# A convolution with batch norm and SiLU: the first weight chunk's three taps loaded in quarters, one behind each of twelve x loads

## The chip, the cores and the metric

The kernel runs on one NeuronCore of a Trainium2 chip. The metric is the device time of one execution in microseconds (us). Beside the timed runs there is one profiled execution, whose trace gives the instructions of each engine, the waits between them and the DMA packets.

## The reference

```python
def reference(x, w, mean, var, g, b):      # x: 2 x 2048 x 1024, w: 3 x 1024 x 1024, bf16
    K = 3
    P = K // 2
    S = x.shape[1]
    xp = jnp.pad(x, ((0, 0), (P, P), (0, 0)))
    y = sum(jnp.einsum('bsc,cd->bsd', xp[:, k:k + S, :], w[k]) for k in range(K))
    inv_std = 1.0 / jnp.sqrt(var + 1e-5)
    y = (y - mean) * (g * inv_std) + b
    return _silu(y)
```

It is a convolution of width 3 along the sequence, over 1024 input and 1024 output channels, for two batches of 2048 positions; then a per-channel scale and shift, and SiLU.

## The kernel before

The convolution is computed in a transformed domain: six outputs of a channel come from eight inputs, with eight products where the direct form has eighteen. A tile is six output positions; a batch has 342 tiles. Each of the eight transformed inputs (j = 0 to 7) is multiplied by its own transformed weights.

**Input side.** A batch is cut into 17 windows of up to 21 tiles: windows of 128 rows of x (256 KB) and a last one of 33 rows. `load_window` (L205) loads one on SP's DMA queue; window 0 of each batch comes in two loads (L211, L212), the others in one (L215). `transform` (L218) turns a window into the transformed domain with TensorE (PE) matmuls against a small constant matrix `Rm` (L225), eight a window for batch 0, and casts the result from PSUM to `T_sb` on ScalarE (ACT, L239) or VectorE (DVE, L241). The pool `xwin` has ten buffers, so a load waits, late in a batch, until PE has read the window ten before it.

**Weight side.** Output channels come in eight chunks of 128. A chunk needs the three raw taps (tap 0, 1, 2: each 128 partitions x 8 channel blocks x 128 columns, 256 KB) and six sums of them, `wts` (the tiles `uch`). j = 0 and j = 7 use raw taps 0 and 2; j = 1 to 6 use the sums. For chunk 0, GpSimd (POOL) makes them: `pair_sum` (L163) adds taps 0 and 2, plain or scaled, `scale_weights` (L149) scales a tap, and `pair_tap` (L173) adds or subtracts tap 1. POOL's order is that of the code: sum, scale tap 2, sum, scale tap 0, sum, then the six products, with tap 1 first read by the first of these. `load_chunk` (L90) loads one tap of one chunk, and its rows in memory are 256 bytes long.

**Order.** Batch 0's loop over 17 windows does nothing on PE but the transforms. Then comes batch 1's loop: between its transforms the matmuls (L250) of the first unit (chunk 0, batch 0) are woven in, about one for every group of two or three transforms, 52 of 64 in all, in the order j = 7, 1, 3, 2, 4, 5, 0, 6. The other fifteen units (a chunk and a batch each) follow, and an output is transposed by DMA and stored on SP's queue behind them. The order on each engine is that of the code; the tile framework adds the waits. All these loads go through SP's one queue. The framework has eight semaphores for DMAs, used in turn, so a load also waits until the one eight places before it has landed.

In batch 0's loop the three taps of chunk 0 are loaded behind windows 3 (tap 0), 5 (tap 2) and 13 (tap 1), each by one load:

```python
            if wi in (3, 5, 13):
                load_chunk(0, {3: 0, 5: 2, 13: 1}[wi])
```

POOL's sums of taps 0 and 2 are written behind window 7, the six products behind window 13.

Of the kernel before, what the change touches and what calls it, by code (L numbers as in the profile page):

```python
# [37 lines left out]
def kernel(  # L38
# [10 lines left out]
    nc = tc.nc  # L49
    B, S, C = x.shape  # L50
    D = w.shape[2]
    P = 128
    CT = C // P
# [19 lines left out]
    w_all = w.rearrange("k (ct p) d -> p k ct d", p=P)  # L73
    raw, wts, wx = {}, {}, {}
# [9 lines left out]
    def load_weights(dp):  # L84
        open_weights(dp)
        for k in (0, 2, 1):
            nc.sync.dma_start(out=pair_tile[dp][:, k], in_=w_all[:, k, :, dp * 2 * P:(dp + 1) * 2 * P])

    def load_chunk(dc, k):
        nc.sync.dma_start(out=raw[dc][k], in_=w_all[:, k, :, dc * P:(dc + 1) * P])  # L90

    open_weights(0)

# [32 lines left out]
    for j in (0, 7):  # L126
        for k in range(NJ):
            if BT[j][k] != 0:
                nc.gpsimd.affine_select(
                    out=Rm[:, j, :],  # L130
                    in_=Rm[:, j, :],
# [12 lines left out]
    def scale_weights(dc, taps=(2, 1, 0), on_gpsimd=False):  # L144
        for k in taps:
            f = 2.0 if k == 1 else 4.0
            dst = wx[dc, k] = wtmp.tile([P, CT, P], BF16, name=f"w{k}x")
            if on_gpsimd:
                nc.gpsimd.tensor_scalar(dst, raw[dc][k], f, 0.0, op0=ALU.mult, op1=ALU.add)  # L149
            else:  # L150
                nc.scalar.mul(dst, raw[dc][k], f)

    def open_chunk(dc):
        wts[dc] = upool.tile([P, 6, CT, P], BF16, name="uch")
# [3 lines left out]
    def pair_sum(dc, n, engine=nc.gpsimd):  # L158

        e = outer[dc, n] = wtmp.tile([P, CT, P], FP32, name=("e1", "e2", "eh")[n])  # L160
        a = wx[dc, 0] if n == 2 else raw[dc][0]
        c = wx[dc, 2] if n == 1 else raw[dc][2]
        engine.tensor_tensor(e, a, c, op=ALU.add)  # L163
# [7 lines left out]
    def pair_tap(dc, n, op):  # L171
        odd = wx[dc, 1] if n else raw[dc][1]
        nc.gpsimd.tensor_tensor(wts[dc][:, 2 * n + (op == ALU.subtract)], outer[dc, n], odd, op=op)  # L173
# [14 lines left out]
    def turn_params():  # L188
        nc.tensor.transpose(prmT.rearrange("p q d -> p (q d)"), prm, ident[0:4 * DC, 0:4 * DC])
        nc.vector.tensor_scalar(rstd, prmT[:, 0, :], 1e-5, 1.0, op0=ALU.add, op1=ALU.mult)  # L190
        nc.gpsimd.tensor_tensor(rstd, rstd, mhalf, op=ALU.pow)

    def make_params():
        nc.vector.tensor_tensor(sc, prmT[:, 1, :], rstd, op=ALU.mult)
        nc.vector.tensor_tensor(beta, prmT[:, 2, :], sc, op=ALU.mult)
        nc.vector.tensor_tensor(beta, prmT[:, 3, :], beta, op=ALU.subtract)
        nc.vector.scalar_tensor_tensor(out=sk, in0=prmT[:, 1, :], scalar=C1, in1=rstd, op0=ALU.mult, op1=ALU.mult)
# [7 lines left out]
    def load_window(xpool, bi, wi):  # L205
        ntile = min(WT, NTB - WT * wi)
        t_lo = M_OUT * WT * wi - 1
        t_hi = min(t_lo + M_OUT * ntile + 1, S - 1)
        kk = t_hi - t_lo + 1
        if t_lo < 0:  # L210
            nc.sync.dma_start(out=xw0[1:113, :], in_=x[bi, 0:112, :])  # L211
            nc.sync.dma_start(out=xw0[113:kk, :], in_=x[bi, 112:t_hi + 1, :])  # L212
            return xw0, kk, ntile
        xw = xpool.tile([P, C], BF16, name="xw")
        nc.sync.dma_start(out=xw[0:kk, :], in_=x[bi, t_lo:t_hi + 1, :])  # L215
        return xw, kk, ntile

    def transform(bi, wi, window, ct0, n, bk, per):  # L218

        xw, kk, ntile = window  # L220
        width = 512 // per if per != 3 else 168
        banks = ps_all[:, bk * 512:(bk + (n + per - 1) // per) * 512]
        for c in range(n):
            at = (c // per) * 512 + (c % per) * width
            nc.tensor.matmul(  # L225
                banks[:, at:at + NJ * ntile],
                lhsT=xw[0:kk, (ct0 + c) * P:(ct0 + c + 1) * P],
                rhs=Rm[0:kk, :, 0:ntile],
                start=True,
                stop=True,  # L230
            )
        src = banks[:, 0:n * width].rearrange("p (s e) -> p s e", e=width)
        src = src[:, :, 0:NJ * ntile].rearrange("p s (j n) -> p s j n", j=NJ)
        dst = T_sb[bi][:, ct0:ct0 + n, :, WT * wi:WT * wi + ntile]
        cost = {e: f + m * n for e, (f, m) in EVAC.items()}
        eng = min(load, key=lambda e: load[e] + cost[e])
        load[eng] += cost[eng]
        if eng == "act":
            nc.scalar.copy(dst, src)  # L239
        else:  # L240
            nc.vector.tensor_copy(dst, src)  # L241
# [97 lines left out]
    def run(gen, n=None):  # L339
        while n is None or n > 0:  # L340
            if next(gen, run) is run:
                return
            if n is not None:
                n -= 1
# [3 lines left out]
    with tc.tile_pool(name="xwin", bufs=10) as xpool:  # L348
        for wi in range(NWIN):
            window = load_window(xpool, 0, wi)  # L350
            if wi in (3, 5, 13):
                load_chunk(0, {3: 0, 5: 2, 13: 1}[wi])
            for h in range(2):
                transform(0, wi, window, 4 * h, 4, (2 * wi + h) % 4 * 2, 2)
            if wi == 0:
                turn_params()
            if wi == 7:
                open_chunk(0)
                for n, taps in ((0, ()), (1, (2,)), (2, (0,))):
                    scale_weights(0, taps, on_gpsimd=True)  # L360
                    pair_sum(0, n)
            if wi == 13:
                pair_tap(0, 0, ALU.add)
                scale_weights(0, (1,), on_gpsimd=True)
                for n, op in ((1, ALU.add), (0, ALU.subtract), (1, ALU.subtract), (2, ALU.add), (2, ALU.subtract)):
                    pair_tap(0, n, op)
        make_params()
        first = unit(0, 0, 0, NTB, (0, 1, 2, 3), yTs[0], late, seven_first=True)
        load["act"] = load["dve"] = 0.0
        gi, done = 0, 0  # L370
        for wi in range(NWIN):
            window = load_window(xpool, 1, wi)
            if wi == 10:
                for k in (0, 2, 1):
                    load_chunk(1, k)
            for ct0, n in ((0, 3), (3, 3), (6, 2)):
                transform(1, wi, window, ct0, n, 4 + gi % 4, 3)
                gi += 1
                want = 52 * max(gi - 1, 0) // (3 * NWIN - 1)
                run(first, want - done)  # L380
                done = want
        load_weights(1)
        run(first)
# [68 lines left out]
    dc, bi = units[-1]  # L452
# [148 lines left out]
```

## Time and profile before

| | |
|---|---|
| median of 3 timed runs | 193.27 us (192.41 to 194.06) |
| profiled execution | 193.53 us |
| its span, first to last instruction | 191.7 us |
| mean granted TensorE clock | 0.975 |
| PE busy | 180.0 us (94% of the span), 1404 matmuls |
| PE weight loads | 128.0 us (67%) |
| DVE busy | 161.3 us (84%) |
| POOL busy | 148.0 us (77%) |
| ACT busy | 122.6 us (64%) |
| DMA | 31.72 MB, mean 165 GB/s |

How to read the profile: engines are PE (matmul), PEld (PE's weight load, which overlaps matmuls), DVE, ACT, POOL and SP; SPq is SP's queue of DMA issues. L215 is line 215 of the kernel. The page gives busy tenths in 40 equal slices of the span. A line of a timeline has the start and the duration in us, the engine, the line of code, the operation, out<-in, how many were merged, and in brackets the idle time before it and what ended that. The chain of waits follows the work that ended last back from the end, and lists it in order of time. Times in them count from the start of the span.

### The profile page before, as it was taken

What the parts mean: (1) busy time and instruction counts of PE and PEld (TensorE: products, weight loads), DVE (VectorE), ACT (ScalarE), POOL (GpSimd) and SP (SyncE); (2) the same over time, 40 slices, a digit from 0 to 9 for tenths busy, and PEclk for the clock granted to TensorE, in tenths of its full rate; (3) what the DMA queues carried; (4) which work ended last, traced back from release to release, by engine and by line L of the source; (5) the groups of instructions that cost most, each with busy time, mean ns of one, the idle gap of its engine ahead of it and who ended that gap; (6) DMA issues with size and microseconds to landing.
All of it is one profiled execution on the core that took longest, in us unless ns stands there. A gap on an engine that the chain in (4) does not pass through costs nothing.

```text
span 191.7 us, 3904 instructions
## 1 busy us (share of the span) xinstructions
PE 180.0 (94%) x1404; PEld 128.0 (67%) x1404; DVE 161.3 (84%) x347; ACT 122.6 (64%) x201; POOL 148.0 (77%) x89
## 2 busy tenths in 40 slices
PE   7579999999999999999999999999999999999960
PEld 3369688866666666666666666666666666669950
DVE  6557999987999699969996999699969987788981
ACT  3747878888287726873786287638755873635770
POOL 6359999999949996999699969996999699900000
PEclk9966999999999999999999999999999999999996
DMA  4999997990608387999292989783746465566425
GB/s 124 323 369 305 329 292 202 285 221 0 123 0 170 69 184 196 275 142 202 46 192 57 205 228 243 147 180 68 168 81 151 95 143 108 124 120 160 118 66 105
DMA packets 86759, 31.72 MB, mean 165 GB/s; under 512 B 73364, under 2 KB 82580, under 8 KB 86740
## 3 DMA queue, kind: packets, MB, share of 16 engines
q1 hardware_dynamic: 86637, 31.46, 70.1%
q8 instruction: 11, 0.18, 0.4%
q14 instruction: 8, 0.07, 0.1%
q10 hardware_dynamic: 103, 0.02, 0.0%
HBM read 14.82 MB, written 8.39 MB: 121 GB/s over the span
## 4 chain that ended last, share of the span: by engine, by line
PE 84%; DVE 6%; DMA 5%; ACT 2%; SPq 1%; issue 1%; DVEq 0%; ACTq 0%
PE ps_all L250 75%; PE ps_all L225 8%; DMA xw<-in_x_dram 5%; DVE T_sb L241 3%; ACT yT L261 1%; DVE y L487 1%; PE ps_all L465 1%; SPq L215 1%; DVE y L291 0%; SPq L90 0%; DVE d L487 0%; DVE ps_all L487 0%; DVE o_end L568 0%; ACT s L507 0%; ACT m L501 0%
## 5 line engine op out<-in xcount | busy, mean ns | idle before, releaser
L250 PE MATMUL ps_all<-T_sb,uch 128*128 128x342 bf16 (+2 forms) x816 | 123.0, 299 | 0.0
L250 PEld LDWEIGHTS <-uch 128*128 128x128 bf16 x816 | 77.0, 97 | 33.2 <-issue 0.2
L261 ACT ACTIVATE yT<-y,beta,sk 128x684 bf16<-128x684 f32 (+5 forms) x46 | 44.2, 960 | 30.3 <-DVE y L291 29.6
L250 PE MATMUL ps_all<-T_sb,wch 128*128 128x342 bf16 (+2 forms) x272 | 44.0, 300 | 0.2 <-DVE T_sb L241 0.2
L291 DVE SCALAR_TENSOR_TENSOR y<-ps_all,y 128x342 f32<-128x342 f32 x90 | 41.9, 507 | 1.7 <-PE ps_all L250 0.7
L173 POOL TENSOR_TENSOR uch<-e,wch 128x1024 bf16<-128x1024 f32 x16 | 33.8, 2134 | 10.8 <-PE ps_all L250 5.9
L173 POOL TENSOR_TENSOR uch<-e,w1x 128x1024 bf16<-128x1024 f32 x16 | 33.8, 2135 | 0.6
L225 PE MATMUL ps_all<-Rm,xw 128*128 128x168 bf16 (+1 forms) x272 | 31.2, 251 | 3.2 <-DMA xw<-in_x_dram 2.8
L173 POOL TENSOR_TENSOR uch<-eh,w1x 128x1024 bf16<-128x1024 f32 x16 | 33.8, 2132 | 0.6
L250 PEld LDWEIGHTS <-wch 128*128 128x128 bf16 x272 | 25.6, 97 | 11.5 <-DVE T_sb L241 0.4
L239 ACT CAST T_sb<-ps_all 128x672 bf16<-128x672 f32 (+5 forms) x45 | 26.3, 606 | 9.4 <-PE ps_all L225 8.3
L298 ACT COPY m<-ps_all 128x342 f32<-128x342 f32 x45 | 19.9, 442 | 19.0 <-PE ps_all L250 18.3
L241 DVE CAST T_sb<-ps_all 128x672 bf16<-128x672 f32 (+3 forms) x40 | 26.3, 698 | 5.6 <-PE ps_all L225 5.2
L225 PEld LDWEIGHTS <-xw 128*128 128x128 bf16 (+1 forms) x272 | 24.6, 106 | 8.5 <-DMA xw<-in_x_dram 3.5
L291 DVE SCALAR_TENSOR_TENSOR y<-ps_all,d 128x342 f32<-128x342 f32 x45 | 20.3, 507 | 0.5
L163 POOL TENSOR_TENSOR e<-wch,w2x 128x1024 f32<-128x1024 bf16 x8 | 17.0, 2130 | 0.2
L163 POOL TENSOR_TENSOR eh<-w0x,wch 128x1024 f32<-128x1024 bf16 x8 | 17.1, 2132 | 0.1
L291 DVE SCALAR_TENSOR_TENSOR y<-ps_all,s 128x342 f32<-128x342 f32 x30 | 14.0, 508 | 3.2 <-ACT s L298 3.2
L291 DVE SCALAR_TENSOR_TENSOR d<-m,ps_all 128x342 f32<-128x342 f32 x15 | 7.6, 507 | 9.3 <-ACT s L298 9.3
L291 DVE SCALAR_TENSOR_TENSOR ps_all<-m,ps_all 128x342 f32<-128x342 f32 x30 | 15.3, 509 | 0.0
L169 DVE TENSOR_REDUCE e<-wch 128x1024 f32<-128x2048 bf16 x6 | 13.7, 2277 | 0.0
L298 ACT COPY s<-ps_all 128x342 f32<-128x342 f32 x30 | 13.1, 438 | 0.0
(65 smaller groups left out, 83.4 us busy)
## 6 DMA issues: line engine op xcount, KB each, us to landing
xw<-in_x_dram SPq DMA_DIRECT2D x30, 256.0 KB
out_dram<-o_sb SPq DMA_DIRECT2D x30, 192.0 KB
wch<-in_w_dram SPq DMA_DIRECT2D x9, 512.0 KB
out_dram<-o_sb SPq DMA_DIRECT2D x15, 120.0 KB
wch<-in_w_dram SPq DMA_DIRECT2D x6, 256.0 KB
xw<-in_x_dram SPq DMA_DIRECT2D x2, 224.0 KB
out_dram<-o_sb SPq DMA_DIRECT2D x15, 7.5 KB
out_dram<-o_sb SPq DMA_DIRECT2D x15, 0.5 KB
```

What stands on the lines that cost most here:

```text
L163: engine.tensor_tensor(e, a, c, op=ALU.add)
L169: nc.vector.tensor_reduce(e, taps.rearrange("p k ct d -> p ct d k"), axis=mybir.AxisListType.X, op=ALU.add)
L173: nc.gpsimd.tensor_tensor(wts[dc][:, 2 * n + (op == ALU.subtract)], outer[dc, n], odd, op=op)
L215: nc.sync.dma_start(out=xw[0:kk, :], in_=x[bi, t_lo:t_hi + 1, :])
L225: nc.tensor.matmul(banks[:, at:at + NJ * ntile], lhsT=xw[0:kk, (ct0 + c) * P:(ct0 + c + 1) * P], rhs=Rm[0:kk, :, 0:ntile], start=True, sto ...
L239: nc.scalar.copy(dst, src)
L241: nc.vector.tensor_copy(dst, src)
L250: nc.tensor.matmul(ps_all[:, bk * 512:bk * 512 + c1 - c0], lhsT=lhsT, rhs=T_sb[bi][:, ct, j, c0:c1], start=start and ct == 0, stop=ct == C ...
L261: nc.scalar.activation(yT[:, i0:i1:step, c0:c1], y_all[:, i0:i1:step], ACT.Silu, bias=beta[:, dc:dc + 1], scale=sk[:, dc:dc + 1],)
L291: nc.vector.scalar_tensor_tensor(out=o, in0=i0, scalar=s, in1=i1, op0=ALU.mult, op1=op1)
L298: nc.scalar.copy(dst, src)
L465: nc.tensor.transpose(pv[0:n1 - n0, ENDS[k]], yT[:, k, n0:n1], ident)
```

## The change

`load_chunk` can load a range of channel blocks. Behind each of the x loads 1 to 12 of batch 0 one load brings two of the eight channel blocks of one tap (64 KB): the four quarters of tap 2 behind windows 1 to 4, those of tap 0 behind 5 to 8, those of tap 1 behind 9 to 12. So twelve loads stand where three were; the bytes are the same, and so is the row length of 256 bytes. The block that issues POOL's sums stands behind window 8 in place of window 7.

```diff
-    def load_chunk(dc, k):
-        nc.sync.dma_start(out=raw[dc][k], in_=w_all[:, k, :, dc * P:(dc + 1) * P])
+    def load_chunk(dc, k, c0=0, c1=CT):
+        nc.sync.dma_start(out=raw[dc][k][:, c0:c1], in_=w_all[:, k, c0:c1, dc * P:(dc + 1) * P])
...
             window = load_window(xpool, 0, wi)
-            if wi in (3, 5, 13):
-                load_chunk(0, {3: 0, 5: 2, 13: 1}[wi])
+            if 1 <= wi < 13:
+                tap, part = divmod(wi - 1, 4)
+                load_chunk(0, (2, 0, 1)[tap], part * CT // 4, (part + 1) * CT // 4)
...
-            if wi == 7:
+            if wi == 8:
                 open_chunk(0)
```

## The prediction

> **What bounds the kernel now.** I read the page's busy shares and slices first, then the chain of waits, then engine timelines and one-microsecond stretches of the first 45 us.
>
> The page, slices of 4.8 us:
>
> ```profile
> PE   7579999999999999999999999999999999999960
> ...
> PEclk9966999999999999999999999999999999999996
> ```
>
> From the fourth slice on TensorE (PE) is full. It is short of work only in the first three, and its clock drops only in the third and fourth. The change touches loads issued in the first 14 us, so all it can do is move the end of the opening; behind that PE has the same instructions in the same order. The chain of waits over the opening (start us, us, what):
>
> ```profile
> 5.98 6.35 DMA xw<-in_x_dram
> 12.33 0.04 issue
> 12.38 5.79 PE ps_all L225 x40
> 18.17 0.02 issue
> 18.20 3.93 DVE T_sb L241 x5
> ```
>
> First an x load is late, then PE itself, then the evacuations, and from 23 us on PE. PE's clock in one-microsecond stretches (us, busy of PE, PEld, DVE, ACT, POOL, PEclk, DMA share, GB/s):
>
> ```profile
> 8.00:9.00 1.00, 0.00 (x1) 0.00 (x0) 0.74 (x1) 0.75 (x2) 0.00 (x0) 1.00 1.14 312
> 9.00:10.00 1.00, 0.16 (x3) 0.17 (x4) 0.00 (x0) 0.00 (x0) 0.00 (x0) 1.00 1.18 284
> ...
> 12.00:13.00 1.00, 0.62 (x5) 0.62 (x6) 0.00 (x0) 0.14 (x1) 1.00 (x1) 0.50 1.03 381
> ...
> 17.00:18.00 1.00, 1.00 (x10) 1.00 (x8) 0.86 (x1) 0.61 (x2) 0.93 (x2) 0.50 1.09 355
> ```
>
> PE is idle around 8 to 10 us while the DMA engines are full: x window 4 waits behind tap 0, and window 6 (12.38) behind tap 2. From 11.4 to 18.2 us the granted clock is 0.50: a window's eight matmuls start 0.14 us apart, not 0.073. What else carries the sum, from the timelines of POOL, PE and SP:
>
> ```profile
> 11.80 2.12 POOL L163 TENSOR_TENSOR e<-wch 128x1024 f32<-128x1024 bf16 x1 [3.87 <-DMA wch<-in_w_dram]
> ...
> 23.68 0.39 PE L225 MATMUL ps_all<-Rm,xw 128*128 128x168 bf16 x3
> ...
> 5.51 0.43 SPq L90 DMA_DIRECT2D wch<-in_w_dram  x1
> ```
>
> POOL's weight work starts when tap 2 lands; 23.68 is the first matmul of batch 1's window 1; an issue of a tap costs SP 0.43 us.
>
> **Sizes of a load.** Landing times below are the trace's semaphore records of each load (a load is spread over 16 engines and has landed when the last reports). Loads of x that follow one another land about 0.68 us apart. A 256 KB tap, in rows of 256 bytes, adds 1.11 us on the engine that reports first (tap 2: 8.77 to 9.88), so a quarter is 0.28 us and a pair, x and quarter, 0.96 us. From tap 0 on one engine runs 1.3 us behind the rest (its tap 0 took 2.32 us where the first took 1.19), and everybody waits for that one. On the first engine loads end without gaps until 18 us: the stream is full, so the order changes but not the total. Before, x windows 4 to 9, 12 and 13 landed at 9.79, 10.57, 12.33, 13.01, 13.67, 14.35, 16.42, 17.18 us.
>
> **The loads rearranged.** Window 3 landed at 6.79; now two quarters are ahead of it: 7.35. Window 4: plus 0.96 and the late engine's 1.13: 9.44. Then 0.96 each: window 5 10.4, 6 11.35, 7 12.3, 8 13.25, 9 14.2, 12 17.1, 13 18.0. So 4 to 8 come 0.2 to 1.0 us earlier, 12 and 13 0.7 and 0.8 us later, and from window 14 on the same bytes are ahead as before.
>
> **PE in the opening.** Windows 4 and 5 give it 1.2 us of work (16 x 0.073) in the 3.4 us ahead of 11.37, where it had about 1.5 us and the clock fell; I take it that it falls again. Windows 6, 7, 8 then start at 11.4, 12.5 and 13.6 at the slow rate (8 x 0.14 = 1.12 us each) and leave no gap, so the clock can return near 14.8 instead of 18.2. From there PE takes windows as they land and ends batch 0 near 21 us instead of 22.3. That is worth up to 1.3 us, but only up to the next late load. Batch 1's window 1 landed at 23.63 and PE began it at 23.68: 0.05 us of slack. The late engine is on its own work until then (window 0's first part 21.42, and a 16 KB instruction fetch of 1.07 us that begins at 20.97, if it runs on that engine, which the records do not tell), and that work is not smaller. What is late next is thus this load, and I book **-0.05 us**, with -1.3 as the far end.
>
> The Trainium skill (TensorE: Matmul & The Clock Gate, Part 1) says that the clock is judged over free-running stretches of about 3.4 us and halves after an idle one. The trace has changes at 4.54, 11.37 and 18.19 us, 6.83 apart, which agrees; but the fall at 11.37 came after a stretch with 45% of matmul, not an idle one. By the rule to the letter the clock would stay up in the changed kernel and batch 0 end near 21 us all the same, held by the loads; the sum would not move.
>
> **Nine more loads.** Each adds a completion packet (9 ns for those of 4 bytes in the trace) to every engine and an issue to SP. If the DMA engines stay the bound, that is 9 x 0.01 = 0.1 us; if SP's issue becomes the bound, 9 x 0.43 = 3.9 us at most. An x issue without a wait takes 0.43 us, a tap's 0.43, with 0.04 between: 0.94 us a pair against 0.96 us of transfer. It just fits; the nearest row is the full stream, so I take **+0.1 us**. Behind each waiting issue on SP stand only the later x and tap loads, and later those of batch 1; the first transpose of an output is at 47.8 us.
>
> **Waits.** A load waits for the landing of the one eight places before. Eight held up to 2 MB; now they hold four pairs, 1.25 MB, 3.84 us of transfer. A load with little ahead took 2.76 us from issue to landing (window 0), the next 3.65 us: the round still fits. I cost it at nothing; without that cover the rival below applies.
>
> **POOL.** Its first sum needs taps 2 and 0 whole, now the quarter behind window 8: 13.25 + 0.28 = 13.5 us, against 11.67, so the chain starts near 13.7, +1.9 us. The order on POOL is unchanged. Who waits: the first unit's matmuls. Tap products ended at 22.66, 25.89, 27.97 and 30.07; PE used them at 25.94, 28.62, 31.37 and 33.84. The least slack is 2.73 us, over 1.9: nothing. Tap 1's last quarter (17.4) is before POOL's use of it (20.5 + 1.9). For the second chunk, POOL's products end at 52.6 and 54.7 with PE at 56.5 and 58.8, and POOL then sits idle 2.8 us, which takes the shift up. Moving the block from window 7 to 8 in the code changes no engine's order, since POOL has nothing between.
>
> **Sum.** -0.05 + 0.1 + 0 + 0 = +0.05 us on the profiled execution's 193.53 us (span 191.7): 193.6. The median of the runs shown is 0.26 below that execution, so **193.3 us**.
>
> **The rivals.**
> 1. *The clock's gain is kept: faster.* If the late engine is less late in the timed runs, window 1 of batch 1 does not hold PE, and ending batch 0 near 21 instead of 22.3 us is kept: 0.5 to 1.3 us, 192.0 to 192.8. For it: on the engine that reports first that window landed at 19.91. Against: the lateness begins and grows in the profiled run beside fetches that the change does not touch. 17%.
> 2. *Eight in flight: slower.* Place: SP's waits on landings, windows 5 to 12 of batch 0. Price: if a round of eight takes 3.65 us and one issue, 4.1 us, three rounds lose 3 x 0.26 = 0.8 us; if issues also queue (1.1 us a pair, as where an x issue took 0.90), 12 x 0.14 = 1.7 us. It decides once a round passes 3.84 us; then window 1 of batch 1, with 0.05 us of slack, is as late: 194.1 to 195.0. Against: the late engine has three pairs, 2.9 us, queued whenever an issue is released. 14%.
> 3. *Weights late: slower.* POOL must start after 11.80 + 2.73 = 14.5 us for it to matter. With pairs of 1.1 us the quarter lands at 15 and the stall is 0.6 us: 193.9, or, with rival 2, 195.5. 6%.
> 4. *It evens nothing.* The late engine loses the same 1.3 us, the clock falls and returns as before, and all is as it was: 193.3 to 193.6, inside the forecast's band. 8%.
> 5. A page's rule speaks against the change as a mechanism of the loads: each small load pays its own latency. Here that is a queue that runs empty between pairs: 2.76 us per load, shared by eight in flight, 0.35 us each, 9 x 0.35 = 3.1 us: 196.4. The rows speak against it: 0.68 us between landings with eight in flight. 4%.
>
> The Trainium skill (DMA: Bandwidth & Descriptors, Rules for kernel authors) is the page for the fifth: small transfers should be joined, since below 64 KB one pays mostly overhead; the quarters are 64 KB exactly. By its fixed cost of about 2.0 us, shared by eight, the sum would be 9 x 0.25 = 2.3 us. No load of 64 KB is in this trace.
>
> **How the numbers follow.** The forecast, 192.8 to 193.8, has 48%, and the fourth lies within it; 3% are for what I have not seen. The range goes out to the first rival's far end and most of the second's: **191.9 to 194.9**. Within 1% (191.3 to 195.2; about what a measurement here can tell from no change) lie the forecast, the fourth, nearly all of the first and much of the second and third: 0.79. Slower by over 1%: the fifth, the ends of the second and third, and the unseen: 0.15. Faster by over 1% needs more than the 1.3 us that the opening has to give, so the first rival's far end and scatter of the runs (192.41 to 194.06) on top: 0.06.
>
> **What would show it.** In the changed profile: PE's idle before window 6 gone, the clock back a slice part earlier (near 15 us); POOL's first sum at 13.5 to 14 us; no wait of PE for weights near 28 us; PE waiting for x ahead of batch 1's window 1 near 23.6 us; 0.94 to 1.0 us per pair on SP. I am wrong if SP's pairs are 1.1 us or more apart, if the clock falls a second time after 15 us (cold windows cost 1.12 us each against 0.68 to land), or if batch 1's window 1 lands elsewhere than 23.6.

## The result and the profile after

The changed kernel takes 195.08 us (median of six runs, 193.94 to 196.50), the kernel before, run beside it, 192.59 us (191.47 to 194.06). The ratio is 1.0135, with a 95% interval of 1.0099 to 1.0171 (the two medians alone give 1.0129): slower by a little over 1%. The prediction (193.3, range 191.9 to 194.9) is wrong: 195.08 lies above its range.

The profiled execution of the changed kernel took 195.03 us, its span 193.2: 1.5 us more than before. The page, slices of 4.8 us:

```profile
PE   7766899999999999999999999999999999999960
...
PEclk9999699999999999999999999999999999999997
```

The low clock stands in the fifth slice, where it stood in the third and fourth. The chain of waits over the opening (start us, us, what):

```profile
5.75 4.83 DMA xw<-in_x_dram
10.58 0.02 issue
10.60 3.80 DMA xw<-in_x_dram
14.40 0.05 issue
14.44 0.08 PE ps_all L225
14.53 5.45 DMA xw<-in_x_dram
19.98 0.05 issue
20.02 3.54 PE ps_all L225 x24
```

Before, an x load ended the chain's DMA part at 12.33 us. Now x loads carry it to 19.98: windows 5, 9 and 13, the second issued when the first landed, the third 0.13 us after the second landed. Then come 24 matmuls in 3.54 us, 0.147 us each: windows 13 to 15 at half clock. TensorE's (PE's) timeline shows the last wait and where batch 1's window 1 begins:

```profile
17.74 0.75 PE L225 MATMUL ps_all<-Rm,xw 128*128 128x168 bf16 x8 [0.45 <-DMA xw<-in_x_dram]
20.02 4.40 PE L225 MATMUL ps_all<-Rm,xw 128*128 128x168 bf16 x38 [1.53 <-DMA xw<-in_x_dram]
...
25.21 0.38 PE L225 MATMUL ps_all<-Rm,xw 128*128 128x168 bf16 x3
```

That window began at 23.68 before and begins at 25.21 now, 1.53 us later: the whole difference of the two spans, and all of it made ahead of this point. The difference of the medians is larger than that of the profiles since the profiled run of the kernel before had a long fall of the clock, and 193.53 us against a median of 192.59.

The six microseconds from 12 to 18 us, first of the kernel before, then of the changed one (us, busy of PE, PEld, DVE, ACT, POOL, PEclk, DMA share, GB/s):

```profile
12.00:18.00 6.00, 5.62 (x41) 5.62 (x42) 3.44 (x4) 3.36 (x6) 5.78 (x4) 0.50 1.10 352
```

```profile
12.00:18.00 6.00, 4.44 (x50) 3.21 (x48) 4.96 (x6) 4.51 (x7) 3.98 (x3) 1.00 0.95 290
```

The stream of loads has become thin: 290 GB/s in place of 352, 0.37 MB less in six microseconds, which is one microsecond of stream at before's rate. SP's timeline shows what SP waited for ahead of it (issues only):

```profile
8.93 0.39 SPq L215 DMA_DIRECT2D xw<-in_x_dram  x1
9.36 0.43 SPq L90 DMA_DIRECT2D wch<-in_w_dram  x1
10.60 0.33 SPq L215 DMA_DIRECT2D xw<-in_x_dram  x1
10.98 0.43 SPq L90 DMA_DIRECT2D wch<-in_w_dram  x1
11.63 0.33 SPq L215 DMA_DIRECT2D xw<-in_x_dram  x1
```

SP is not busy between 9.79 and 10.60. Window 9's load goes out at 10.60 because window 5's, eight places ahead, landed at 10.58; window 10's at 11.63, after window 6's at 11.61; windows 7 and 8 the same (7.99 after 7.97, 8.93 after 8.91). From issue to landing the loads of windows 5 to 12 took 3.7 to 4.9 us, and eight places (the eight semaphores, one for each load on the way) held 3.84 us of transfer. The first of the 16 engines reported each of these loads after 2.4 to 3.1 us; a place is free only when the last has.

Waiting for a landing is not new: in the first 20 us SP waited 5.0 us in all for landings in the kernel before, and 2.4 us here. But there up to eight loads of 256 KB were on the way meanwhile. Here the DMA engines' share of busy time fell to 0.81 from 9 to 10 us and to 0.80 from 13 to 14.

### The profile page after: what moved, and what is told of

Same layout as the page of the kernel before. It is cut to its first block, busy times and chain, and to the rows that moved or that the text cites. A ratio compares the mean times of both kernels' runs of the same rounds, so it can differ in the third digit from the quotient of the medians.

```text
span 193.2 us, 3916 instructions
## 1 busy us (share of the span) xinstructions
PE 179.8 (93%) x1404; PEld 126.8 (66%) x1404; DVE 162.0 (84%) x347; ACT 123.0 (64%) x201; POOL 148.0 (77%) x89
## 4 chain that ended last, share of the span: by engine, by line
PE 81%; DMA 9%; DVE 4%; ACT 2%; SPq 1%; issue 1%; DVEq 0%; ACTq 0%
PE ps_all L250 75%; DMA xw<-in_x_dram 9%; PE ps_all L225 6%; DVE T_sb L241 1%; ACT yT L261 1%; DVE y L488 1%; PE ps_all L466 1%; SPq L90 1%; SPq L215 0%; DVE y L291 0%; DVE d L488 0%; DVE ps_all L488 0%; DVE o_end L569 0%; ACT s L508 0%; ACT m L502 0%
## 5 line engine op out<-in xcount | busy, mean ns | idle before, releaser
L173 POOL TENSOR_TENSOR uch<-e,wch 128x1024 bf16<-128x1024 f32 x16 | 33.8, 2133 | 10.3 <-PE ps_all L250 5.4
L241 DVE CAST T_sb<-ps_all 128x672 bf16<-128x672 f32 (+3 forms) x40 | 27.0, 700 | 6.4 <-PE ps_all L225 5.7
L298 ACT COPY m<-ps_all 128x342 f32<-128x342 f32 x45 | 19.9, 443 | 18.8 <-PE ps_all L250 18.2
L225 PEld LDWEIGHTS <-xw 128*128 128x128 bf16 (+1 forms) x272 | 23.4, 104 | 11.2 <-DMA xw<-in_x_dram 7.3
L169 DVE TENSOR_REDUCE e<-wch 128x1024 f32<-128x2048 bf16 x6 | 13.7, 2276 | 0.0
```

The lines of the kernel that those rows point to most:

```text
L169: nc.vector.tensor_reduce(e, taps.rearrange("p k ct d -> p ct d k"), axis=mybir.AxisListType.X, op=ALU.add)
L225: nc.tensor.matmul(banks[:, at:at + NJ * ntile], lhsT=xw[0:kk, (ct0 + c) * P:(ct0 + c + 1) * P], rhs=Rm[0:kk, :, 0:ntile], start=True, sto ...
```

## The experiments

Two theories, after the two things seen. **Thin stream**: nine more loads in SP's queue keep too few bytes on the way, so x lands late. **Late clock fall**: PE, now fed at the pace of the loads, has a poor stretch near 18 us, the clock falls at 20 us, and three windows at half rate push the first unit. Rivals: cutting a tap into 64 KB pieces costs by itself; the place of the bytes (tap 1 ahead of window 13) does it; POOL's later start does it. All ratios are against runs of the kernel before on the same chip. The GB/s are those of the DMA engines from 12 to 18 us and from 0 to 22 us; "window 1" is PE's first matmul on batch 1's window 1; times are in us. These columns and the last are from one profiled run each.

| kernel | ratio (95%) | GB/s, 12 to 18 | GB/s, 0 to 22 | batch 0's window 15 landed | window 1 | clock at half |
|---|---|---|---|---|---|---|
| before | 1 | 352 | 286 | 20.41 | 23.68 | 11.4 to 18.2 |
| changed | 1.0135 (1.0099 to 1.0171) | 290 | 263 | 21.78 | 25.21 | 20.0 to 23.4 |
| whole taps behind 4, 8, 12 | 1.0036 (1.0005 to 1.0067) | 344 | 276 | 20.75 | 23.21 | none |
| halves | 1.0045 (1.0009 to 1.0082) | 347 | 282 | 20.35 | 22.81 | none |
| quarters, but tap 2 in halves behind 3, 4 | 1.0103 (1.0027 to 1.0179) | 294 | 267 | 21.04 | 23.50 | none |
| tap 1 whole | 1.0155 (1.0133 to 1.0177) | 321 | 268 | 20.78 | 23.75 | 21.7 to 25.1 |
| before + nine tiny loads | 1.0179 (1.0113 to 1.0246) | 259 | 250 | 22.69 | 25.96 | 11.5 to 15.0, 21.8 to 25.2 |
| changed + extra matmuls | 1.0096 (1.0081 to 1.0111) | 338 | 267 | 21.23 | 24.11 | none |
| before + extra matmuls | 1.0060 (1.0037 to 1.0082) | 343 | 288 | 20.19 | 22.84 | none |
| before, tap 1 behind 16 | 1.0048 (1.0006 to 1.0090) | 349 | 289 | 18.01 | 21.96 | none |
| tiny loads on ACT | 1.0153 (1.0094 to 1.0213) | 335 | 271 | 18.80 | 25.31 | 10.3 to 17.1 |
| quarters on POOL | 1.0188 (1.0112 to 1.0264) | 313 | 284 | 20.53 | 23.07 | none |
| before + a few extra matmuls | 1.0000 (0.9969 to 1.0032) | 347 | 286 | 20.57 | 23.03 | none |

Two things hold across the rows. Behind the start of window 1, what is left of the span is 168.0 to 168.6 us in ten of the thirteen profiles, so what differs between these kernels is made ahead of that point. The three others are tap 1 whole (169.2, the first unit at half clock), halves (169.3, with a wait of 0.88 us for x at 34.15 us) and quarters on POOL (171.0, with waits for weights of 2.07 us; the rest of its loss was not traced). And the kernels with nine to twelve loads of weights or of nothing in SP's queue move 250 to 268 GB/s over the first 22 us, those with six or fewer 276 to 289, other than the tiny loads on ACT (271). The profiled run of the kernel before is one of its longer ones: its window 1 waited for a load that landed at 23.63 us.

### Whole taps in the changed kernel's places

```diff
-            if 1 <= wi < 13:
-                tap, part = divmod(wi - 1, 4)
-                load_chunk(0, (2, 0, 1)[tap], part * CT // 4, (part + 1) * CT // 4)
+            if wi in (4, 8, 12):
+                load_chunk(0, {4: 2, 8: 0, 12: 1}[wi])
```

> The three taps whole again, but at the ends of their four quarters' places: tap 2 behind window 4, tap 0 behind 8, tap 1 behind 12, POOL's sums behind window 8. At the end of each group the same bytes are ahead as in the changed kernel, with three loads in place of twelve. Thin stream (twelve more places among the eight in flight starve the DMA engines between 12 and 15 us): the stream is full again, so the time is within 0.5 us of the kernel before. Place (tap 1 ahead of window 13, POOL's start later): still 1.5 to 2.5 us slower than before. Late clock fall: slower by 1.3 us or more only if the clock falls after 17 us again.

1.0036, 0.7 us: a quarter of the loss, a little over the 0.5 us that the thin stream allowed, with the stream nearly full again (344 GB/s). The same bytes are ahead of window 13 as in the changed kernel, so place is not the cause. POOL started at 13.94 us, 0.07 later than in the changed kernel (13.87), and PE's first-unit matmuls ran without a gap for it: POOL's later start is not the cause either.

### Tap 1 whole behind window 13

```diff
-            if 1 <= wi < 13:
+            if 1 <= wi < 9:
                 tap, part = divmod(wi - 1, 4)
-                load_chunk(0, (2, 0, 1)[tap], part * CT // 4, (part + 1) * CT // 4)
+                load_chunk(0, (2, 0)[tap], part * CT // 4, (part + 1) * CT // 4)
+            if wi == 13:
+                load_chunk(0, 1)
```

> Quarters of taps 2 and 0 behind windows 1 to 8 as in the changed kernel, but tap 1 whole behind window 13, as before the change. Thin stream: windows 9 to 13 follow each other 0.68 us apart again, window 13 lands near 17.5 us in place of 19.98, and the time is within 0.7 us of the kernel before. Late clock fall: the same, if the clock does not fall after 17 us; if the pairs of 1 to 8 are what matters, 1.5 us or more slower than before. POOL's late start (1.9 to 2.1 us) is the same as in the changed kernel, so if that alone were the cause nothing is won.

The expectation missed. Window 13 landed at 17.29 us as expected of the thin stream, and the stream was better from 12 to 18 us (321 GB/s), yet the kernel is as slow as the changed one, and over the first 22 us it moved little more (268 GB/s against 263). In the profiled run the clock fell at 21.7 us, and from there the first unit itself began at half rate; the mean clock of all four runs was 0.979 to 0.981. The stretch ahead of that fall (columns as above):

```profile
18.31:21.72 3.41, 1.65 (x24) 1.31 (x24) 1.71 (x3) 1.40 (x3) 3.26 (x3) 1.00 1.05 263
```

PE was busy 1.65 of 3.41 us, 48%: it had no windows in store and waited 1.25 us for window 14 and 0.74 us for window 15.

### PE kept busy: extra matmuls in both kernels

```diff
             for h in range(2):
+                if wi >= 3:
+                    bk = (2 * wi + h) % 4 * 2
+                    nc.tensor.matmul(ps_all[:, bk * 512:bk * 512 + 336], lhsT=warm[:, 0:P], rhs=warm[:, 0:336],
+                                     start=True, stop=True)
                 transform(0, wi, window, 4 * h, 4, (2 * wi + h) % 4 * 2, 2)
```

On the changed kernel:

> The changed kernel with one extra matmul of zeros (336 columns, 0.14 us at full clock) ahead of each half of windows 3 to 16 of batch 0; it writes a PSUM bank that the transform then overwrites. PE is kept busy while it waits for x. Late clock fall: the clock stays at full rate, windows 13 to 15 run in 0.6 us each in place of 1.12, and 1.2 to 1.7 us of the 2.5 come back. Thin stream: the x loads land as late as in the changed kernel, and at most 0.4 us comes back.

On the kernel before:

> The kernel before with the same extra matmuls. If the fall of the clock between 11.4 and 18.2 us costs the kernel before nothing, because batch 1's window 1 lands at 23.6 us anyway, the time stays within 0.3 us; if it costs what the opening seemed to give, 0.5 to 1.3 us faster.

In the changed kernel the clock stayed up and the ratio went from 1.0135 to 1.0096, 0.75 us: less than the 1.2 to 1.7 us expected, more than the thin stream alone allowed. The intervals overlap, and the extra matmuls cost something: on the kernel before they cost 0.6%, where faster or no change was expected. The clock's part of the loss is thus, as an estimate, some 0.75 us, or more by what the extra matmuls cost here, which was not measured apart. The profile of the changed kernel fits an estimate of that size: window 15 landed at 21.78 us, its eight matmuls would take 0.58 us at full rate (0.073 each), so they would end near 22.4, and they ended at 23.56. The six timed runs agree too: the two with a mean clock of 0.992 and more took 193.94 and 194.44 us, the four with 0.971 to 0.987 took 195.03 to 196.50. Those two runs are still over a microsecond above the median of the kernel before, with the clock up: that part goes with the loads.

The profile of the changed kernel with the extra matmuls shows one thing more. The loads are those of the changed kernel, but from 3.86 to 11.72 us SP never waited for a place; it issued without a pause, a pair every 0.99 us, and window 9 went out at 9.80 us, after window 5 had landed at 9.61 (issues only):

```profile
9.80 0.47 SPq L215 DMA_DIRECT2D xw<-in_x_dram  x1
10.31 0.43 SPq L90 DMA_DIRECT2D wch<-in_w_dram  x1
10.78 0.47 SPq L215 DMA_DIRECT2D xw<-in_x_dram  x1
```

From 12 to 18 us the stream was not thin (338 GB/s), but from 10 to 12 us it was (261 GB/s), and why it was is not known; over 22 us it moved 267 GB/s, little more than in the changed kernel (263). So the late loads come back with the load count, and the wait for a place at 9.79 us does not.

### Nine loads of nothing

```diff
             if wi in (3, 5, 13):
                 load_chunk(0, {3: 0, 5: 2, 13: 1}[wi])
+            if wi in (1, 2, 4, 6, 7, 8, 9, 10, 11):
+                tiny = consts.tile([16, 64], BF16, name=f"tiny{wi}")
+                nc.sync.dma_start(out=tiny, in_=w[0, 0:16, 0:64])
```

> The kernel before, its three whole taps where they were, and nine loads of 2 KB into tiles that nobody reads, one behind each of the x windows 1, 2, 4 and 6 to 11: as many loads on SP as in the changed kernel, none of its other moves. Thin stream (each extra load takes SP's issue time and one of the eight places, and the DMA engines run empty at the start and from 12 to 15 us): 1.0 to 2.0 us slower than before, window 15 landing about 1 us later. If it is the cutting of the taps itself or POOL's late start: within 0.4 us of before.

The ratio is 1.0179 (1.0113 to 1.0246): the kernel before, its taps whole and where they were, is slowed as much as by the change, or more, by nine loads that carry 18 KB in all. The six microseconds from 12 to 18 and SP's issues:

```profile
12.00:18.00 6.00, 5.51 (x50) 4.92 (x51) 4.05 (x6) 4.17 (x7) 5.78 (x4) 0.75 0.88 259
```

```profile
10.46 0.33 SPq L215 DMA_DIRECT2D xw<-in_x_dram  x1
11.58 0.33 SPq L355 DMA_DIRECT2D tiny<-in_w_dram  x1
12.25 0.33 SPq L215 DMA_DIRECT2D xw<-in_x_dram  x1
```

The DMA engines' share falls to 0.88 and the rate to 259 GB/s. Window 9's load was issued at 10.46 after window 5's landed at 10.44, window 10's at 12.25 after window 6's at 12.23. A 2 KB load holds one of the eight places until it has come through the queue behind the x loads (2.2 to 4.5 us from issue to landing), so the same places hold fewer bytes. PE then waited 2.44 us for window 14:

```profile
21.88 2.42 PE L225 MATMUL ps_all<-Rm,xw 128*128 128x168 bf16 x16 [2.44 <-DMA xw<-in_x_dram]
```

So the load count in SP's queue is enough to cause a loss of this size, with nothing else of the change in it. The clock follows here too: the stretch ahead of the second fall had PE busy 30%.

### Six loads in place of twelve, and a free start

```diff
-            if 1 <= wi < 13:
-                tap, part = divmod(wi - 1, 4)
-                load_chunk(0, (2, 0, 1)[tap], part * CT // 4, (part + 1) * CT // 4)
+            if 1 <= wi < 13 and wi % 2 == 0:
+                tap, part = divmod(wi // 2 - 1, 2)
+                load_chunk(0, (2, 0, 1)[tap], part * CT // 2, (part + 1) * CT // 2)
```

> The taps in halves of four channel blocks, six loads, behind windows 2, 4, 6, 8, 10 and 12, in the changed kernel's order; the same bytes are ahead of each even window's successor. Thin stream: between the whole taps at 4, 8, 12 (0.4% slower than before) and the quarters (1.4%): 0.5 to 1.0% slower. If a threshold decides (a round of eight longer than the transfer it covers), as good as the whole taps.

The second kernel keeps the quarters of taps 0 and 1, but loads tap 2 in two halves behind windows 3 and 4:

```diff
-            if 1 <= wi < 13:
+            if wi in (3, 4):
+                load_chunk(0, 2, (wi - 3) * CT // 2, (wi - 2) * CT // 2)
+            if 5 <= wi < 13:
```

> The changed kernel with tap 2 in two halves behind windows 3 and 4; the quarters of taps 0 and 1 stay behind 5 to 12. The first three windows are issued as in the kernel before, without a wait for a place among the eight. If the hole at the start (DMA engines at 0.78 of their time between 5 and 6 us, window 3 at 7.97 in place of 6.79) is what is lost, about 0.5 us come back and the time is 0.9 to 1.1% above before; if the stretch from 12 to 15 us counts alone, at most 0.2 us.

Halves cost 0.45% (347 GB/s), whole taps in the same places 0.36%: going from three loads to six costs nothing that these intervals can tell, and nine, ten and twelve loads cost 1.0 to 1.8%. That is nearer to a threshold than to a price per load. It is what places would do, which cost once the round of eight is longer than the transfer that it holds; SP's issue time would do it as well, once a pair of issues takes longer than the pair's transfer. The free start brings window 3 back to 6.71 us (7.97 in the changed kernel) and the ratio to 1.0103, 0.3 points as expected, though the interval is wide; from 12 to 18 us the stream is as thin as in the changed kernel (294 GB/s).

### Places or issue time

The nine tiny loads from ACT's queue (`nc.scalar` in place of `nc.sync` in the kernel above):

> The nine tiny loads of the earlier run (1.8% slower on SP's queue), now issued by ACT between its casts: they take places among the eight as before, but none of SP's issue time. If the places are what starves the stream, x loads still wait for a load that is few x loads ahead, and the time is 1.0% or more above before, though a tiny load on a queue of its own lands sooner and may free its place early (then 0.5 to 1.0%). If SP's issue time (0.43 us each) is what starves it, the time is within 0.4% of before.

This decides nothing. The stream stayed full (335 GB/s, window 15 at 18.80 us), but ACT issued only two of the nine ahead of 12 us: now ACT stood still for a place ahead of its casts, and PE for ACT:

```profile
PE ps_all L225 <- ACT T_sb L239: 4.0, 5, 1.8
ACT T_sb L239 <- DMA xw<-in_x_dram: 3.4, 2, 2.8
```

The time was lost in another way (the view is that of the waits: us in total, times, longest).

The x windows 5 to 12 two at a time, with the quarters kept:

```diff
+                if wi % 2:
+                    two = xpair.tile([P, 2, C], BF16, name="xpair")
...
+                    nc.sync.dma_start(out=two, in_=both)
+                    for part in (wi - 1, wi):
+                        load_chunk(0, (2, 0, 1)[part // 4], part % 4 * CT // 4, (part % 4 + 1) * CT // 4)
```

> The changed kernel, its twelve quarters kept, but the x windows 5 to 12 loaded two at a time (512 KB a load, the two quarters behind it), with fewer window buffers (six single, three double). From window 5 on the eight places hold some 5.1 us of transfer in place of 3.84, more than the 3.7 to 4.5 us that a load takes from issue to landing. If the places starve the stream: the DMA engines stay full from 8 us on, over 4.85 MB have moved by 18 us (changed kernel 4.61, before 5.10), and the time is 0.3 to 0.8% above before. If cutting the taps into 64 KB pieces is what costs: no gain, 1.2 to 1.5% above before.

The ratio is 1.037 (1.0291 to 1.0450), where 0.3 to 1.5% was expected, and this decides nothing either: with the fewer window buffers the fourth double load went out at 13.54 us only, once PE had read the first pair, and batch 1's loads waited for buffers too (its window 3 was issued at 22.40 us, before at 18.58). The buffers starved it.

The quarters of taps 2 and 0 issued by POOL at the start, tap 1 whole behind window 13:

```diff
+            if wi == 0:
+                for tap in (2, 0):
+                    for part in range(4):
+                        c0, c1 = part * CT // 4, (part + 1) * CT // 4
+                        nc.gpsimd.dma_start(out=raw[0][tap][:, c0:c1], in_=w_all[:, tap, c0:c1, 0:P])
+            if wi == 13:
+                load_chunk(0, 1)
```

> The quarters of taps 2 and 0 issued by POOL at the start, by its own descriptor path, which has its own semaphores; tap 1 whole on SP behind window 13. SP issues only x and tap 1 and all eight places are x's. The kernel with these quarters on SP was 1.55% slower than before. If cutting the taps costs (eight 64 KB pieces), still 1% or more slower. If places and issue on SP cost, within 0.5% of before; faster than before only if the taps, no longer ahead of window 4 in the queue, let x land steadily, up to 0.4%.

The ratio is 1.0188 (1.0112 to 1.0264), as slow as it should be if cutting the taps were the cost, but the time was not lost in the stream: batch 1's window 1 began at 23.07 us, earlier than in the profile of the kernel before. POOL's eight issues took 5.95 us, the last quarters landed at 16.1, and the weights were late:

```profile
16.28 2.13 POOL L163 TENSOR_TENSOR e<-wch 128x1024 f32<-128x1024 bf16 x1 [4.27 <-DMA wch<-in_w_dram]
```

```profile
27.18 0.32 PE L250 MATMUL ps_all<-T_sb,uch 128*128 128x342 bf16 x1 [1.70 <-POOL uch L173]
...
30.40 0.32 PE L250 MATMUL ps_all<-T_sb,uch 128*128 128x342 bf16 x1 [0.37 <-POOL uch L173]
```

This is the third rival of the prediction, and it begins to cost where the prediction put it: POOL starting at 16.28, past 14.5 us, makes PE wait 2.07 us in all, where the prediction's sum gives 1.8. And with taps 2 and 0 cut into the same eight pieces of 64 KB, x came about as in the kernel before (window 15 at 20.53 against 20.41, 284 GB/s over 22 us against 286): cutting a tap is not what makes x late, having the pieces in SP's queue does. Whether the place counts there or the issue of 0.43 us stays open. In the profiles of the changed kernel and of the nine tiny loads SP stood idle until the landing eight loads ahead; in that of the changed kernel with extra matmuls it issued without a pause until 11.72 us. No run separates the two.

### Two tries at a faster kernel

Tap 1 behind window 16 in place of 13, with POOL's products behind it:

```diff
-            if wi in (3, 5, 13):
-                load_chunk(0, {3: 0, 5: 2, 13: 1}[wi])
+            if wi in (3, 5, 16):
+                load_chunk(0, {3: 0, 5: 2, 16: 1}[wi])
```

> The kernel before with tap 1 whole behind window 16 in place of 13, and POOL's six products with it. If the landing of batch 0's last windows sets when the first unit starts, these land 1.1 us earlier and up to 0.8 us is gained; if batch 1's window 1 sets it, with the same bytes ahead as before, nothing; if POOL's wait for tap 1 (then at about 21 us, needed at 20.5) is passed on through 2.7 us of slack, still nothing.

Window 15 landed at 18.01 us, 2.4 us earlier than before, and PE then waited 1.26 us for batch 1's first window:

```profile
21.09 0.60 PE L225 MATMUL ps_all<-Rm,xw 128*128 128x168 bf16 x6 [1.26 <-DMA xw<-in_x_dram]
```

Batch 1's loads are the next limit, as the prediction had it. The median is 0.5% slower; four runs with a mean clock of 0.989 and more took 191.88 to 192.66 us, five of the other six (0.982 to 0.986) took 193.5 and over.

Four extra matmuls ahead of windows 4, 6, 14 and 15 of the kernel before:

```diff
+            for _ in range(4 if wi in (4, 6, 14, 15) else 0):
+                bk = 2 * wi % 4 * 2
+                nc.tensor.matmul(ps_all[:, bk * 512:bk * 512 + 336], lhsT=warm[:, 0:P], rhs=warm[:, 0:336],
+                                 start=True, stop=True)
```

> The kernel before with four extra matmuls of zeros (336 columns, 0.14 us each) ahead of windows 4, 6, 14 and 15 of batch 0 alone, where PE waits for x behind a tap. In all profiles so far the clock fell after each 3.41 us stretch with PE busy 48% or less, and after none with 51% or more; 0.56 us more work in a wait adds 16% to such a stretch. If falls of the clock are what sets the kernel before's slower runs (193 us and more), these go and the median is 0 to 0.3% faster; if the x stream alone sets the end, the same within 0.2%; if PE does not wait there in undisturbed runs, the extra work costs up to 0.5%.

There is no difference (0.9969 to 1.0032). No kernel that ran is faster than the one before.

## Why the prediction was wrong, by its own steps

**What bounds the kernel** held: the change can only move the end of the opening, and the whole difference of the spans is there at 25.21 us.

**The loads rearranged**: windows 4 to 8 were forecast at 9.44, 10.4, 11.35, 12.3 and 13.25 us and landed at 8.91, 10.58, 11.61, 12.50 and 13.48. Up to there the sizes are right. Then 12 came at 17.69 (17.1) and 13 at 19.98 (18.0). One engine reported 1.4 us after the others for window 13; in the kernel before one did so at tap 0. What holds it up was not found, and a 16 KB instruction fetch that begins at 16.88 is only a candidate.

**Nine more loads and Waits** are the steps that failed: +0.1 us and nothing, where the loads cost over a microsecond. The words "the round still fits. I cost it at nothing" took the time from issue to landing from the first loads, 2.76 and 3.65 us, issued into an empty queue. For windows 5 to 12 of the changed kernel it was 3.7 to 4.9 us, and the eight places hold 3.84 us. "It just fits", 0.94 us of issues a pair against 0.96 us of transfer, was as close: SP took 0.99 us a pair where it issued without a wait, and from window 7 to window 13, with the waits, 1.09 us on average. Six pairs at 0.13 us over the transfer are 0.8 us. The second rival had this place, this price (0.8 to 1.7 us) and this deciding point, at 14%; its argument against itself, that the late engine always has 2.9 us queued, forgot the other fifteen: the engines' mean share fell to 0.80, and the stream to 290 GB/s. Which of the two steps weighs more stays open, as said above.

**The fifth rival**, 2.76 us shared by eight, gave 0.35 us a load and 3.1 us in all, and the nine tiny loads cost 1.8%, 3.4 us, 0.38 us each. That the sizes are near is in part luck: a fall of the clock is in the 3.4 us, and a price for each load is not what the runs show, since halves, with three loads more than whole taps, cost 0.1% more and not 0.5%. The Trainium skill (DMA: Bandwidth & Descriptors, Rules for kernel authors) counts loads under 64 KB as mostly overhead. The prediction's estimate of 2.3 us rests on a fixed cost of about 2.0 us, which the same page of the Trainium skill gives where it describes loads issued by GpSimd (Anatomy of one DMA — SWDGE (gpsimd) path); these were issued by SP. 2.5 us was measured, near it by the same luck.

**PE in the opening** was wrong on where the clock falls. I forecast a fall at 11.37 as before and a return near 14.8. There was none: from 6.33 to 16.57 us PE was busy 77, 62 and 71% of each stretch, evenly fed as the change means it to be. The fall came at 19.99, behind a stretch of 43%, where three windows still had to run and nothing behind them could take the loss. The prediction named a fall after 15 us as a way to be wrong but gave it no chance and no term in the sum; by the estimates above it is worth 0.75 to 1.2 us.

**-0.05 us for batch 1's window 1**: this load landed at 23.19 us, but PE was not there until 25.21, so the edge never came into play here. That batch 1's loads can hold PE is shown by the run with tap 1 behind 16, though there it was window 0.

**POOL** was right: it started at 13.87 (13.7 forecast) and nobody waited. The slack of 2.73 us was confirmed from the other side, by the run that passed it.

## What to carry to other kernels

Count the loads that are added to a queue, and not only their bytes: nine loads of 2 KB among large ones cost as much here as nine more pieces of the weights. Two sums bear on whether they fit. The first holds the time from issue to landing on the last engine against the transfer time of as many loads as may be on the way; the first loads of a trace, issued into an empty queue, give too low a time for it. The second holds the issue time of a pair against its transfer time. Where either comes out within a few per cent, as both did here, it is a risk to be priced and not a zero. And a PE that is fed evenly at 60 to 70% has no work in store, so one late load close to the end can cost itself and a fall of the clock.

## What the runs showed of the hardware

The clock changes at times that lie a whole number of 3.41 us apart (6.33, 19.99 and 23.40 us in the changed kernel, four stretches and one; 4.54, 11.37 and 18.19 before, two and two), and the phase of these stretches differs from run to run. Over all fourteen profiles (the thirteen of the table and that of the double loads), taken up to 27 us, the clock fell behind each of the eight stretches at full rate with PE busy 48% or less (28, 30, 43, 44, 45, 47, 48, 48%) and behind none with 51% or more. At half rate it came back behind stretches of 78% and more, not behind two of 71 and 73%. Two lines on either side of the bar, the changed kernel and whole taps (columns as above):

```profile
16.57:19.99 3.42, 1.48 (x16) 1.06 (x16) 2.20 (x3) 1.58 (x3) 3.27 (x3) 1.00 1.01 325
```

```profile
7.53:10.94 3.41, 1.75 (x21) 1.44 (x22) 1.87 (x3) 1.72 (x3) 0.21 (x1) 1.00 1.04 346
```

The first, 43%, was followed by a fall, the second, 51%, was not. The Trainium skill (TensorE: Matmul & The Clock Gate, Part 1) has the clock halve after an idle stretch. These runs differ: a stretch with PE busy 48% was enough, so the bar lies near half busy here.
